# A stream of operands that runs ahead by free memory, and raw weights loaded a pass ahead of their sums

## The chip, the cores and the metric

The kernel runs on one core of one Trainium2 chip. Its five engines work from queues of their own and wait for each other by semaphores: TensorE (PE) multiplies, VectorE (DVE) and ScalarE (ACT) work on elements, GpSimd (POOL) does a little arithmetic and issues most stores, SyncE (SP) issues the loads. The metric is the device time of one execution in microseconds, lower is better.

## The reference

Four residual sublayers in turn: Fourier mixing, gated feed-forward, mixing, feed-forward, each on a layer-normalised input of 2048 rows and 512 columns, all in float32.

```
a = z @ dft_hid_re.T ; b = z @ dft_hid_im.T        # z = layernorm(x), 2048 x 512
x = x + (dft_seq_re @ a - dft_seq_im @ b)          # 2048 x 2048 matrices
x = x + (gelu(z @ w_gate) * (z @ w_up)) @ w_down   # 512 x 1792, 1792 x 512
```

## The kernel before

**Arithmetic.** A float32 operand v is divided into two parts that TensorE takes at its full rate: hi, a rounded copy written by ACT (L110), and lo = v - hi, written by DVE (L111). Each product is then three matmuls, hi by hi, hi by lo and lo by hi (`mm3`, L144 to L146), on operands of 128 x 128 and 128 x 512. The large products are done in blocks of two by two with seven products instead of eight. This needs sums and differences of operands ahead of the products (`plus`, L135, and `minus`, L132, both on DVE) and of results after them; the latter read PSUM by L135 (DVE) or are copied out of it by L139 (ACT). Such an instruction, which frees a PSUM bank that a later product needs, is called an evacuation below. The first block of layer 0 uses plain float32 matmuls instead (L551), and transposes stand at L454.

**Memory.** SBUF is 102 slots of 128 x 512 (`Slots`): `get` takes the slot that has been free longest, `put` gives one back. A load therefore waits for the last reader of the slot that it gets. Eight PSUM banks are handled in the same way.

**The stream.** All operands from outside, in the order of their use, are one list of items for the whole kernel: the rows of the sequence matrices (`ws`, A11, A12, S2, S3, A22 of four blocks in each mixing layer), the hidden matrices (`wh`), and the two parts of each down weight (`wd`). An item has its addresses and a function that makes its parts: for `ws` rows a split, for S2 rows three sums or differences and a split; a down weight was divided long before and passes as it is. `load_next` (L210) issues the loads of the next item on SP; `split_next` makes the parts of the next item, after loading up to RAW = 4 further items; `take`, called by each product, makes items up to AHEAD = 5 ahead of the one it returns:

```
    while stream["split"] <= min(n + AHEAD, len(items) - 1):
        ...
        split_next()
```

**Small jobs.** `queue` holds small jobs, one of which is run by `step()` at each product: normalising rows of x, block sums, and the preparation of weights. `weight_steps(n)` prepares gate and up weight n (14 of them): a load of the raw weight (three DMAs of `wgu`, L664 to L666, on SP behind the stream's last load), its four sums (L135, L132), and four jobs that split a piece each and store the parts (`kept`, L197, on POOL) for the three later passes, which load them ready made (`weight_load`, L712). Weights 0 and 1 are prepared in the last block of layer 0's mixing, weights 2 to 13 during the first pass of layer 1 (`geglu(0, 1)`), where `up(n)` works on weight n. There are two passes (halves of the rows) in each feed-forward layer. At the end of `up(n)` stands

```
    if making and n + 3 < NF:
        queue.extend(weight_steps(n + 3))
```
so that the load, the sums and the splits of weight n + 3 are consecutive jobs during `up(n + 1)`. Gates go through L722 to L725 (ACT, DVE, ACT, DVE) and L739 (DVE).

**Order.** A scheduler reads this program and fixes the order of the instructions on each engine before the run. On the chip each engine works through its queue strictly in that order, so an instruction whose operand is late holds up all behind it on the same engine. SP issues loads in program order.

Of the kernel before, what the change touches and what calls it, by code (L numbers as in the profile page):

```python
# [10 lines left out]
F32R = mybir.dt.float32r  # L11
# [7 lines left out]
NF = F // P  # L19
# [6 lines left out]
AHEAD = 5  # L26
RAW = 4
WARM = 16
LAG = 6
EARLY = 2  # L30
SKEW = 2
NSLOT = 102
# [6 lines left out]
def fnet_geglu(ctx: ExitStack, tc: tile.TileContext, x_in, ws, wh, wgu, wdn, out):  # L39
# [63 lines left out]
    sb = Slots(slots, "s", NSLOT)  # L103
    ps8 = Slots(psum, "p", 8)

    def f32(ap):
        return ap.bitcast(F32)
# [82 lines left out]
    wds = {f: dram.tile([P, 1024], F32, name=f"wd{f}") for f in range(NF)}  # L190

    def halves(t):
        return t[:, :512], t[:, 512:]
# [6 lines left out]
    items = []  # L200
    stream = {"loaded": 0, "split": 0, "used": 0}
    raws, parts = {}, {}

    def load_next():
        n = stream["loaded"]
        dtype, addresses, _, _ = items[n]
        raws[n] = []
        for a in addresses:
            t = sb.get(dtype)
            stream["last"] = nc.sync.dma_start(t if dtype == F32 else f32(t), a)  # L210
            raws[n].append(t)
        stream["loaded"] += 1

    def split_next():
        n = stream["split"]
        while stream["loaded"] <= min(n + RAW, len(items) - 1):
            load_next()
        parts[n] = items[n][2](*raws.pop(n))
        stream["split"] += 1

    def take():
        n = stream["used"]
        while stream["split"] <= min(n + AHEAD, len(items) - 1):
            need = items[stream["split"]][3]
            if need and need not in cs and stream["split"] > n:
                break
            split_next()
        stream["used"] += 1
        return parts.pop(n)

# [5 lines left out]
    s1s, s2s, s3s, cs, held = {}, {}, {}, {}, {}  # L236

    def as_is(v):
        return (v,)

    def make_a11(k):

# [110 lines left out]
    for layer in range(0, 4, 2):  # L353
        mix_items(layer)
        for _ in range(NB // 2):
            items.extend((F32R, halves(wds[f]), lambda *w: w, None) for _ in range(2) for f in range(NF))


    queue = []
# [147 lines left out]
    def mix(layer):  # L507
        hid, sums = {}, {}
# [69 lines left out]
                    cs[0, c] = v  # L578
            ps8.put(*side)

        chains, sides, us, ws4 = {}, {}, {}, {}

        def s2(b):
            last, fore = b == NB - 1, b < FORE[layer]
            if fore:
                chains[b] = [ps8.get() for _ in range(2)]
                if b:
                    sums[b] = [fetched((layer, b, c)) for c in range(2)]
                    cs.update({(0, c): fetched((layer, b, c, "sum")) for c in range(2)})
            chain, side = chains[b], [ps8.get() for _ in range(2)]  # L590
            sides[b] = side
            if last and layer == 0:
                queue.extend(weight_steps(0))
            for second, k in skewed():
                if second:
                    six(side, "T1", k, k == 0, k == NK - 1, "T12" if last else None)
                else:
                    six(chain, "T2", k, fore and k == 0, k == NK - 1)
            us[b] = [based(b, c, p) for c, p in enumerate(chain)]
            ws4[b] = [based(b, c, p) for c, p in enumerate(side)]  # L600

        def s3(b):
            last = b == NB - 1
            chain, side, u, w4 = chains[b], sides.pop(b), us.pop(b), ws4.pop(b)
            if last:
                queue.extend(block_steps(layer + 1, 0))
                if layer == 0:
                    queue.extend(weight_steps(1))
            for second, k in skewed():
                if second:  # L610
                    six(side, "B22", k, False, k == NK - 1, "2" if last else None)
                else:
                    six(chain, "T3", k, False, k == NK - 1)
                if not second and k == NK - 1:
                    for c in range(2):
                        plus(w4[c], w4[c], chain[c])
                        cs[1, 2 + c] = w4[c]
            for c in range(2):
                plus(u[c], u[c], side[c])
                cs[0, 2 + c] = u[c]  # L620
            ps8.put(*side)
# [27 lines left out]
    pieces = (("A11", "A12"), ("S2", "S3"), ("S1", "A22"), ("S4",))  # L649
# [4 lines left out]
    def weight_steps(n):  # L654

        src, v = [], {}

        def load():
            src.extend(sb.get() for _ in range(4))
            for i, names in enumerate((*pieces[:3], ("S4", "A21"))):  # L660
                for name, h in zip(names, half):
                    v[name] = src[i][:, h]
            with tc.issue_after(stream["last"].ins):
                nc.sync.dma_start(src[0], wgu[n, :, :512])  # L664
                nc.sync.dma_start(v["A22"], wgu[n, :, 512:768])
                nc.sync.dma_start(v["A21"], wgu[n, :, 768:])  # L666

        def sums():
            plus(v["S1"], v["A21"], v["A22"])
            minus(v["S2"], v["S1"], v["A11"])  # L670
            minus(v["S3"], v["A11"], v["A21"])
            minus(v["S4"], v["A12"], v["S2"])

        def divide(i):
            def run():
                to = wblocks[n][:, i * 1024:min((i + 1) * 1024, 7 * 512)]
                p = wparts.setdefault(n, {"tiles": []})
                if i < 3:
                    t = split_slot(src[i])
                    kept(to, t)  # L680
                    for name, h in zip(pieces[i], half):
                        p[name] = (t[0][:, h], t[1][:, h])
                else:
                    t = (split_side(v["S4"]),)
                    nc.gpsimd.dma_start(to, f32(t[0]))
                    p["S4"] = (t[0][:, half[0]], t[0][:, half[1]])
                p["tiles"] += t
                sb.put(src[i])
            return run

        return [load, sums] + [divide(i) for i in range(len(pieces))]

    def down_weight_steps(f):

# [33 lines left out]
    def geglu(w, layer):  # L728
# [30 lines left out]
                yield  # L759
            sb.put(*hs, *v)  # L760

        making = layer == 1 and w == 0


        chain, side, c11, u, w4 = {}, {}, {}, {}, {}
# [1 line left out]
        def product(n, ps, an, bn, start, stop):  # L767
            if making:
                step()
            hi, lo = wparts[n][an]  # L770
            for c in range(2):
                cut = slice(c * P, (c + 1) * P)
                mm3(ps, (hi[:, cut], lo[:, cut]), blocks[bn, c], start and c == 0, stop and c == 1)
# [15 lines left out]
                sb.put(v)  # L789

        def up(n, down):
            product(n, chain[n], "S2", "T2", False, True)
            u[n] = copied(chain[n])
            next(down, None)
            side[n] = ps8.get()
            product(n, side[n], "S1", "T1", True, True)
            w4[n] = copied(side[n])
            next(down, None)
            first(n + 1)
            product(n, chain[n], "S3", "T3", False, True)  # L800
            v = w4.pop(n)
            plus(v, v, chain[n])
            finished(n, 1, 1, v)
            sb.put(v)
            next(down, None)
            product(n, side[n], "S4", "B22", False, True)
            v = u.pop(n)
            plus(v, v, side[n])
            ps8.put(side.pop(n))
            finished(n, 0, 1, v)  # L810
            sb.put(v)
            next(down, None)
            second(n + 1)
            product(n, chain[n], "A22", "T4", False, True)
            ps = chain.pop(n)
            if n % 2 == 0:
                v = copied(ps)
                finished(n, 1, 0, v)
                sb.put(v)
            else:  # L820
                finished(n, 1, 0, ps)
            ps8.put(ps)
            for _ in down:
                pass
            sb.put(*wparts.pop(n)["tiles"])
            if making and n + 3 < NF:
                queue.extend(weight_steps(n + 3))
            elif not making and n + 2 < NF:
                weight_load(n + 2)

        def down(f, part):
# [24 lines left out]
                x_add(layer, (w * 2 + 1) * NT + i, xrows.pop(0), acc[1][i], engine=nc.sync)  # L856

        before_mix = w == 1 and layer < 3
        if making:
            queue.extend(weight_steps(2))  # L860
        first(0)
        second(0)
        for n in range(NF):
            up(n, down_steps(n - LAG, 0) if n >= LAG else iter(()))
        for bc in list(blocks):
            sb.put(*blocks.pop(bc))
        load_rows(0)
        if before_mix:
            queue.extend((lambda k=k: first_rows(layer + 1, k)) for k in range(NK))
        for f in range(NF - LAG, NF):  # L870
            down(f, 0)
# [112 lines left out]
```

## Time and profile before

| | us |
|---|---|
| median of 3 runs (lowest, highest) | 1668.8 (1666.82, 1669.08) |
| the profiled execution | 1666.76 |
| its span, first to last instruction | 1664.9 |
| PE busy | 1650.4 |
| DVE busy | 1190.7 |
| ACT busy | 776.2 |
| median landing of a load of a `ws` row, a `wd` part | 4.0, 4.3 |

The profile is of one execution. A timeline row gives start, duration, engine, line, operation, operands and shape, and in square brackets the idle time of the engine before it and what ended that. Matmuls are drawn longer than the distance of their starts, as they overlap in the array. A row with x2 or more joins that many instructions that follow each other. L12 is line 12 of the kernel before, and `s`, `p`, `x`, `ws`, `wgu`, `wd` are slots, PSUM banks, rows of x, sequence rows, raw gate and up weights, and down weights. In the table by stretches each row is a time window with the busy time and count of each engine.

### The profile page before, as it was taken

What the parts mean: (1) busy time and instruction counts of PE and PEld (TensorE: products, weight loads), DVE (VectorE), ACT (ScalarE), POOL (GpSimd) and SP (SyncE); (2) the same over time, 40 slices, a digit from 0 to 9 for tenths busy, and PEclk for the clock granted to TensorE, in tenths of its full rate; (3) what the DMA queues carried; (4) which work ended last, traced back from release to release, by engine and by line L of the source; (5) the groups of instructions that cost most, each with busy time, mean ns of one, the idle gap of its engine ahead of it and who ended that gap; (6) DMA issues with size and microseconds to landing.
All of it is one profiled execution on the core that took longest, in us unless ns stands there. A gap on an engine that the chain in (4) does not pass through costs nothing.

```text
span 1664.9 us, 22527 instructions
## 1 busy us (share of the span) xinstructions
PE 1650.4 (99%) x7296; PEld 1359.2 (82%) x7296; DVE 1190.7 (72%) x2132; ACT 776.2 (47%) x1352; POOL 169.3 (10%) x288
## 2 busy tenths in 40 slices
PE   9999999999999999999999999999999999999999
PEld 6877788888788888888888888888888888888887
DVE  8997978687887765655898785857946556656561
ACT  7744434255565543534663333444635443444440
POOL 3212100021422110000210000000100000100000
PEclk9999999999999999999999999999999999999999
DMA  9788886778766876555665766565695559755551
GB/s 361 247 279 329 306 317 227 253 252 291 273 229 215 292 269 233 172 189 198 216 227 182 240 228 228 168 227 188 225 386 184 171 177 321 259 178 175 186 183 51
DMA packets 200726, 388.46 MB, mean 233 GB/s; under 512 B 23840, under 2 KB 27424, under 8 KB 200608
## 3 DMA queue, kind: packets, MB, share of 16 engines
q1 hardware_dynamic: 183168, 329.86, 59.1%
q0 software_dynamic: 17440, 57.16, 9.1%
q8 instruction: 58, 0.95, 0.2%
q14 instruction: 60, 0.49, 0.1%
HBM read 328.73 MB, written 58.20 MB: 232 GB/s over the span
## 4 chain that ended last, share of the span: by engine, by line
PE 93%; DVE 3%; DMA 2%; issue 1%; ACT 1%; SPq 0%; DVEq 0%; ACTq 0%
PE p L144 31%; PE p L145 30%; PE p L146 30%; DMA s<-wgu 2%; DVE s L111 1%; PE p L551 1%; PE p L454 1%; DVE s L135 1%; DMA s<-ws 1%; DVE s L132 1%; DMA s<-x 0%; DVE s L725 0%; DVE s L739 0%; DVE s L723 0%; ACT s L110 0%
## 5 line engine op out<-in xcount | busy, mean ns | idle before, releaser
L145 PE MATMUL p<-s,s 128*128 128x512 f32 x2368 | 921.7, 390 | 1.9 <-DVE s L111 1.9
L146 PE MATMUL p<-s,s 128*128 128x512 f32 x2368 | 908.6, 390 | 0.0
L144 PE MATMUL p<-s,s 128*128 128x512 f32 x2368 | 901.2, 391 | 7.0 <-DVE s L135 3.9
L110 ACT ACTIVATE s<-s 128x512 fp32r<-128x512 f32 (+1 forms) x758 | 438.0, 617 | 467.6 <-DVE s L132 98.6
L111 DVE TENSOR_TENSOR s<-s,s 128x512 fp32r<-128x512 f32 (+1 forms) x758 | 490.2, 679 | 87.1 <-ACT s L110 64.3
L144 PEld LDWEIGHTS p<-s,s 128*128 128x128 f32 x2368 | 445.0, 188 | 102.9 <-DVE s L135 5.0
L145 PEld LDWEIGHTS p<-s,s 128*128 128x128 f32 x2368 | 445.4, 188 | 95.0 <-DVE s L111 3.1
L146 PEld LDWEIGHTS p<-s,s 128*128 128x128 f32 x2368 | 445.2, 188 | 93.7 <-DVE s L111 0.7
L135 DVE TENSOR_TENSOR s<-s,p 128x512 f32<-128x512 f32 x316 | 213.0, 685 | 188.9 <-PE p L146 140.6
L139 ACT ACTIVATE s<-p 128x512 f32<-128x512 f32 x248 | 145.2, 593 | 187.4 <-PE p L146 171.4
L132 DVE TENSOR_TENSOR s<-s,s 128x512 f32<-128x512 f32 (+1 forms) x290 | 172.4, 608 | 23.4 <-DMA s<-ws 15.4
L722 ACT ACTIVATE s<-s 128x512 f32<-128x512 f32 x112 | 70.4, 630 | 91.7 <-DVE s L135 90.9
L725 DVE SCALAR_TENSOR_TENSOR s<-s,s 128x512 f32<-128x512 f32 x112 | 76.8, 690 | 38.2 <-ACT s L724 37.6
L378 POOL TENSOR_TENSOR rstd<-rstd,power 128x1 f32<-128x1 f32 x64 | 50.8, 803 | 506.7 <-DVE rstd L377 500.8
L723 DVE SCALAR_TENSOR_TENSOR s<-s,s 128x512 f32<-128x512 f32 x112 | 77.0, 690 | 33.5 <-ACT s L722 31.3
L724 ACT ACTIVATE s<-s 128x512 f32<-128x512 f32 x112 | 69.5, 627 | 25.0 <-DVE s L723 24.4
L135 DVE TENSOR_TENSOR s<-s,s 128x512 f32<-128x512 f32 (+1 forms) x78 | 50.1, 645 | 38.5 <-DMA s<-ws 22.1
L169 POOL DMA_DIRECT2D x<-s x48 | 26.1, 543 | 443.8 <-DVE s L135 440.8
L382 ACT ACTIVATE s<-s,shift,rstd 128x512 f32<-128x512 f32 x64 | 50.4, 811 | 36.5 <-DVE shift L380 32.1
L739 DVE SCALAR_TENSOR_TENSOR s<-s,s 128x512 f32<-128x512 f32 x84 | 58.0, 690 | 1.6
L197 POOL DMA_DIRECT2D wb<-s x84 | 45.2, 540 | 121.6 <-ACT s L110 85.1
L373 DVE BATCH_NORM_STATS2 st<-s 128x6 f32<-128x512 f32 x64 | 42.7, 689 | 19.8 <-DMA s<-x 19.8
(32 smaller groups left out, 254.6 us busy)
## 6 DMA issues: line engine op xcount, KB each, us to landing
s<-ws SPq DMA_DIRECT2D x432, 256.0 KB, 4.0
s<-wb SPq DMA_DIRECT2D x294, 256.0 KB, 4.1
s<-wd SPq DMA_DIRECT2D x224, 256.0 KB, 4.3
s<-x SPq DMA_DIRECT2D x126, 256.0 KB, 4.1
s<-wh SPq DMA_DIRECT2D x120, 256.0 KB, 4.8
wb<-s POOLq DMA_DIRECT2D x98, 256.0 KB, 3.5
x<-s POOLq DMA_DIRECT2D x48, 256.0 KB, 4.1
wd<-s POOLq DMA_DIRECT2D x28, 256.0 KB, 4.9
```

Source lines behind the costliest of these rows:

```text
L110: nc.scalar.activation(hi, src, AF.Copy)
L111: nc.vector.tensor_tensor(lo, src, f32(hi), op=ALU.subtract)
L132: nc.vector.tensor_tensor(out, a, b, op=ALU.subtract)
L135: nc.vector.tensor_tensor(out, a, b, op=ALU.add)
L139: nc.scalar.activation(v, src, AF.Copy)
L144: nc.tensor.matmul(ps, ah, bh, start=start, stop=False, skip_group_check=True)
L145: nc.tensor.matmul(ps, ah, bl, start=False, stop=False, skip_group_check=True)
L146: nc.tensor.matmul(ps, al, bh, start=False, stop=stop, skip_group_check=True)
L722: nc.scalar.activation(t, g, AF.Square)
L723: nc.vector.scalar_tensor_tensor(t, t, 1.0 / GELU_C, g, op0=ALU.add, op1=ALU.mult)
L724: nc.scalar.activation(t, t, AF.Tanh, scale=GELU_A * GELU_C)
L725: nc.vector.scalar_tensor_tensor(t, t, 1.0, g, op0=ALU.add, op1=ALU.mult)
```

## The change

The stream: `take` may make the parts of one further item, up to FAR = 14 ahead of the item it returns, if more than ROOM = 10 slots are free and the item isn't a down weight. Down weights, whose parts need no work, are loaded and held only NEAR = 2 ahead.

The weights: `weight_steps` returns its load apart from its other jobs. In the first pass of layer 1 the load of weight n + 3 is issued at the beginning of `up(n)`, and the sums and splits of weight n + 2 are queued there; before, load, sums and splits of n + 3 were queued together at the end of `up(n)`. The load of weight 2 stands at the start of the pass. The loads of weights 0 and 1 are both queued in the S2 part of layer 0's last block, with the sums and splits of weight 0 behind them; those of weight 1 are queued in the S3 part.

Both kernels issue the same instructions; their order on the engines and the slots that they use differ. Line numbers shift by 3 near the top and by about 15 further down.

```diff
+FAR = 14
+ROOM = 10
+NEAR = 2
...
     def split_next():
         n = stream["split"]
         while stream["loaded"] <= min(n + RAW, len(items) - 1):
+            if stream["loaded"] > n + NEAR and items[stream["loaded"]][2] is whole:
+                break
             load_next()
...
             if need and need not in cs and stream["split"] > n:
                 break
+            if items[stream["split"]][2] is whole and stream["split"] > n + NEAR:
+                break
             split_next()
+        m = stream["split"]
+        if n + AHEAD < m <= min(n + FAR, len(items) - 1) and len(sb.free) > ROOM:
+            if items[m][2] is not whole and (items[m][3] is None or items[m][3] in cs):
+                split_next()
         stream["used"] += 1
         return parts.pop(n)
...
+    def whole(*parts):
+        return parts
...
-            items.extend((F32R, halves(wds[f]), lambda *w: w, None) for _ in range(2) for f in range(NF))
+            items.extend((F32R, halves(wds[f]), whole, None) for _ in range(2) for f in range(NF))
...
         def s2(b):
             if last and layer == 0:
-                queue.extend(weight_steps(0))
+                opening_weights.update((n, weight_steps(n)) for n in range(2))
+                queue.extend([opening_weights[0][0], None, opening_weights[1][0], None, *opening_weights[0][1]])
...
         def s3(b):
                 if layer == 0:
-                    queue.extend(weight_steps(1))
+                    queue.extend(opening_weights[1][1])
...
-        return [load, sums] + [divide(i) for i in range(len(pieces))]
+        return load, [sums] + [divide(i) for i in range(len(pieces))]
...
-        making = layer == 1 and w == 0
+        making = {}
+        if layer == 1 and w == 0:
+            making.update((n, weight_steps(n)) for n in range(2, NF))
+            making[2][0]()
...
         def up(n, down):
+            if n + 3 in making:
+                making[n + 3][0]()
+            if n + 2 in making:
+                queue.extend(making[n + 2][1])
             product(n, chain[n], "S2", "T2", False, True)
...
-            if making and n + 3 < NF:
-                queue.extend(weight_steps(n + 3))
-            elif not making and n + 2 < NF:
+            if not making and n + 2 < NF:
                 weight_load(n + 2)
...
-        if making:
-            queue.extend(weight_steps(2))
```

More of the change, by code (lines that the diff above doesn't have):

```diff
@@ L579, in a12 @@
             ps8.put(*side)
-        chains, sides, us, ws4 = {}, {}, {}, {}
+        chains, sides, us, ws4, opening_weights = {}, {}, {}, {}, {}
         def s2(b):
```

## The prediction

> **What bounds the kernel now.** I read the page's first part, then what PE waited for, then PE's timeline around each of those waits, then the table by stretches, and last the queues behind the waits.
>
> ```profile
> PE 1650.4 (99%) x7296; PEld 1359.2 (82%) x7296; DVE 1190.7 (72%) x2132; ACT 776.2 (47%) x1352; POOL 169.3 (10%) x288
> ```
> ```profile
> engine line waited for: us in total, times, longest us
> PE p L144 <- DVE s L135: 3.9, 3, 2.3
> PE p L144 <- ACT s L139: 2.5, 3, 1.9
> PE p L145 <- DVE s L111: 1.9, 2, 1.1
> PE p L144 <- ACT s L110: 0.6, 1, 0.6
> ```
> PE is the bound: 99% busy, and outside the first microseconds its waits add up to 8.9 us in nine places. Only these can be won, since both kernels issue the same instructions. PE's timeline shows the places and what each really costs:
>
> ```profile
> 88.26 0.50 PE L145 MATMUL p<-s,s 128*128 128x512 f32 x1 [0.83 <-DVE s L111]
> ...
> 109.54 0.74 PE L144 MATMUL p<-s,s 128*128 128x512 f32 x2 [0.58 <-ACT s L110]
> ...
> 128.63 0.50 PE L145 MATMUL p<-s,s 128*128 128x512 f32 x1 [1.12 <-DVE s L111]
> ...
> 203.33 0.80 PE L144 MATMUL p<-s,s 128*128 128x512 f32 x1 [2.30 <-DVE s L135]
> ...
> 206.46 0.40 PE L145 MATMUL p<-s,s 128*128 128x512 f32 x1
> ...
> 208.09 0.40 PE L145 MATMUL p<-s,s 128*128 128x512 f32 x1
> ...
> 211.95 0.39 PE L144 MATMUL p<-s,s 128*128 128x512 f32 x1
> ...
> 356.62 0.50 PE L144 MATMUL p<-s,s 128*128 128x512 f32 x1 [1.02 <-DVE s L135]
> ...
> 441.27 0.50 PE L144 MATMUL p<-s,s 128*128 128x512 f32 x1 [0.47 <-ACT s L139]
> ...
> 444.55 0.50 PE L144 MATMUL p<-s,s 128*128 128x512 f32 x1 [1.85 <-ACT s L139]
> 445.61 0.79 PE L144 MATMUL p<-s,s 128*128 128x512 f32 x1 [0.56 <-DVE s L135]
> ...
> 449.01 0.40 PE L144 MATMUL p<-s,s 128*128 128x512 f32 x1
> ...
> 552.40 0.50 PE L144 MATMUL p<-s,s 128*128 128x512 f32 x1 [0.18 <-ACT s L139]
> ```
> From 208.09 to 211.95 lie 17 matmuls: one starts every 0.227 us, though each is drawn 0.39 long. So a stall costs 0.16 more than the idle time in brackets: 8.91 + 9 x 0.16 = 10.35 us. After two of them PE also restarts slowly: seven matmuls from 203.33 to 206.46 take 3.13 us instead of 1.59, and eight from 445.61 to 449.01 take 3.40 instead of 1.82, together 3.1 us. All that can be won is thus about 13.5 us: 3.0 us by 130, 4.0 at 203, 1.2 at 356, 5.0 at 441 to 449, 0.3 at 552.
>
> The table by stretches (times from:to, then busy us and count of PE, PEld, DVE, ACT, POOL, the granted clock, DMA share, GB/s) tells why:
>
> ```profile
> 41.60:83.20 41.60, 41.60 (x186) 34.43 (x185) 41.15 (x86) 31.04 (x57) 10.27 (x8) 1.00 0.75 247
> 83.20:124.90 41.70, 40.29 (x177) 32.73 (x176) 40.62 (x69) 19.15 (x35) 7.56 (x14) 1.00 0.80 279
> 124.90:166.50 41.60, 40.48 (x179) 33.19 (x178) 31.65 (x52) 18.14 (x32) 11.86 (x22) 1.00 0.89 329
> 166.50:208.00 41.50, 39.20 (x167) 32.02 (x166) 40.42 (x68) 17.82 (x31) 6.48 (x12) 0.96 0.84 307
> ...
> 560.00:1664.00 1104.00, 1101.27 (x4906) 912.16 (x4905) 720.58 (x1255) 484.66 (x836) 52.90 (x88) 1.00 0.63 212
> ```
> DVE is full from 41.6 to 124.9 and from 166.5 to 208, with 10 us idle between: there a PE stall is a place in DVE's queue. From 560 on DVE has a third of its time free and PE has no wait of the list above. Between 403 and 446 the cause is another:
>
> ```profile
> 418.45 0.69 DVE L111 TENSOR_TENSOR s<-s,s 128x512 fp32r<-128x512 f32 x1 [4.80 <-ACT s L110]
> ...
> 436.98 0.43 DVE L135 TENSOR_TENSOR s<-s,s 128x256 f32<-128x256 f32 x1 [4.68 <-DMA s<-wgu]
> ```
> ```profile
> 430.78 7.73 DMA s<-wgu
> ```
> DVE idles 4.80 and 4.68 us at the head of its queue, for a raw gate and up weight that has not landed (the first through ACT's split of it); the chain of waits runs through that transfer. The evacuations queued behind are late at 441 to 446.
>
> **The change, part by part.** The instructions are the same ones in another order, so I counted, on both kernels' instruction lists, how far each operand that PE needs has moved on its producer's queue and how far its matmul has moved on PE. A DVE instruction of 512 columns counts 0.60 us:
>
> ```profile
> 360.14 0.69 DVE L373 BATCH_NORM_STATS2 st<-s 128x6 f32<-128x512 f32 x1
> 360.74 0.68 DVE L135 TENSOR_TENSOR s<-s,p 128x512 f32<-128x512 f32 x1
> ```
>
> *Raw weights a pass earlier.* Weights 2 to 13 of the first GeGLU are loaded about a pass ahead of their sums. The last load of weight 5 was issued here, when its slot came free:
>
> ```profile
> 432.67 0.72 SPq L664 DMA_DIRECT2D s<-wgu  x1
> ```
> In the new order it waits for a matmul that ran 14 us before that, and the loads of weights 2 to 4 are released by work that ran 7 to 12 us before theirs. With the weights there earlier, DVE does their sums where it now idles 4.80 and 4.68 us, and so reaches the evacuations of 441 to 446 up to 9.5 us sooner; these have moved back by only 1.0 us of work, two to three places. The 5.0 us and the 0.3 us at 552 go: **-5.3 us**.
>
> What is late next? The sums of weights 7 to 13 still stand at the head of DVE soon after their loads. In 446 to 560 DVE waits for them today without hurting PE:
>
> ```profile
> DVE s L135 <- DMA s<-wgu: 7.8, 5, 2.9
> DVE s L132 <- DMA s<-wgu: 4.3, 3, 2.6
> ```
> In the new order I count waits of 1.5 to 3 us with at least 1.6 us of slack for the evacuations behind: nothing on the path at the median landing, the fourth rival beyond it.
>
> *Weights 0 and 1 and x0 near 335 to 365.* Weight 1's three loads and its sums move from about 390 into the stretch from 333 where DVE is nearly full. Two rows tell the room there: the evacuation of row 360.74 above, which ended at 361.42, and the matmul that needs it, the second of the two here, at 365.40:
>
> ```profile
> 365.18 0.62 PE L144 MATMUL p<-s,s 128*128 128x512 f32 x2
> ```
> Its slack was 3.99 us. In the new order that matmul stands 38 places earlier, 8.6 us, while its evacuation (no. 568 on DVE, now 564) has only 2.9 us less work ahead. It is late by 8.6 - 2.9 - 3.99 = 1.7 us; and as today's stall of 1.2 us at 356 lies ahead of that matmul and goes, by 2.9 us. That is longer than the 2.30 us after which PE restarted slowly, so 1.5 us come on top. Ends: 0 (DVE has had time to catch up) and 4.4; I take 4.4, since row 203.33 is the nearest in length. Against today's 1.2: **+3.2 us**.
>
> A rule bears on that restart. The microsecond after the idle 2.30 us, with the granted clock behind the five engines:
>
> ```profile
> 203.00:204.00 1.00, 0.67 (x2) 0.58 (x3) 1.00 (x3) 0.00 (x0) 0.49 (x1) 0.51 0.73 293
> ```
> The Trainium skill, "TensorE: Matmul & The Clock Gate", section "Why this matters for your kernels", sets the limit for a halved clock at idle gaps of about 3 us. The trace shows 0.51 after 2.30 us, and the measurement decides; by the page's limit a stall of 2.9 us would restart at full speed, and the sum would be 1.5 us lower (rival 5).
>
> *The stream up to fourteen items ahead, 41 to 130.* The split that PE waited for at 88 moves from no. 190 to 172 on DVE, 10.6 us less work ahead: gone. The one at 109 (ACT) has 2.3 us less, the one at 128 2.4 us less against 1.3: gone. But block 0's later operands pulled ahead stand before earlier ones. An example is the split no. 223, the second of this DVE row, and its matmul:
>
> ```profile
> 106.73 1.33 DVE L111 TENSOR_TENSOR s<-s,s 128x512 fp32r<-128x512 f32 x2
> ```
> ```profile
> 111.48 0.39 PE L145 MATMUL p<-s,s 128*128 128x512 f32 x1
> ```
> The split ends at 108.06, so its slack was 3.4 us; its place on DVE stays, its matmul comes 18 places (4.1 us) earlier: late by 0.7 us. Two neighbours are late by 1.1 and 1.3 by the same count, and the 1.0 us of the stall at 88 that is gone comes on top: 2.3 us in three pieces, none long enough for a slow restart. Ends 0 and 4. So 3.0 becomes 2.3: **-0.7 us**.
>
> *130 to 208.* Block 1's operands are loaded 2 to 16 us earlier. The evacuation of 203.33 stays where it was (no. 358, now 357), but its matmul stands 16 places, 3.6 us, later on PE, against 2.5 us of stall: **-4.0 us** with its restart. In its stead one split (no. 335, now 345) has 6.0 us more work ahead, and a matmul 1.8 us later; the 10 us in which DVE idles in 124.90 to 166.50 cover it. Without that cover it costs up to 3.4 us; I take 0.
>
> *Down weights two items ahead instead of five; the start.* How long a load takes at worst is shown by the nearest kind, the raw weights of L664:
>
> ```profile
> DMA to landing us min/median/max: 2.5/4.7/7.2
> ```
> The shorter lead still leaves 80 matmuls, 18 us, ahead of their use, so 0. At the start the first block's loads go one place ahead of x4 and later rows, 0 to 0.5 us: **+0.3**.
>
> **Sum**: -5.3 + 3.2 - 0.7 - 4.0 + 0.3 = -6.5 us. The profiled execution took 1666.8, so 1660.3; it was 2.0 us under the median of 1668.8, which gives **1662.3**.
>
> **The rivals.**
> 1. *Nothing new is late*: DVE, freed of its waits, reaches 335 to 365 and 97 to 105 in time. For it speaks the idle DVE time in 124.90 to 166.50; against it that DVE is full just before both places. 13.5 - 1.5 = 12 us: 1657.
> 2. *The delays only change place*: besides my 4.4 and 2.3 us the split no. 345 costs its 3.4 and restarts slowly (1.5): -6.5 + 4.9 = -1.6, 1667.2.
> 3. *It does not run ahead*: loads wait for slots anyway, and asking earlier does not free one.
>
> ```profile
> SPq L210 <- PE p L146: 311.8, 201, 7.9
> ```
> Then only places change: 1668 to 1669. Against it: the loads' releasers in the new order are earlier matmuls.
>
> 4. *Slower: the weights' sums block DVE.* A sum at the head of DVE waits for a load issued shortly before; evacuations stand behind. With 1.6 us of slack it costs PE nothing up to a landing of 4.7 + 1.6 = 6.3 us. At 7.2 each of the twelve weights stalls PE by 0.9: 10.8 us, 1673; the change is slower than today from 0.55 us for each. Today's waits of 7.8 and 4.3 us left PE alone, which speaks against. The Trainium skill, "DMA: Bandwidth & Descriptors", section "Latency and other measured facts", allows memory access 2 us at high load instead of 0.2, which as an estimate would reach 6.5; the transfers here run at 0.6 to 0.9 of the engines' time and land as that row says, mostly sooner.
> 5. *The stall near 350 restarts at full speed*, because PE's idle time ends just short of what the clock reacts to: 1.5 us less, 1660.8. Row 203.33 speaks against it, row 128.63 with 1.12 us and no slow restart for it. This is what the page on the clock gate would have.
>
> **How the numbers follow.** My forecast has 0.38 (1659 to 1665), the first rival 0.22, the second and third 0.16 together, the fourth 0.12, the fifth 0.12. Runs of this kernel differ by 0.14%, so about 0.2%, 3.3 us, can be told from no change: below 1665.5 is faster. Forecast, first and fifth rival give faster 0.72, the second and third same 0.16, the fourth slower 0.12. The range leaves out the fourth and the ends of the others: 1655.5 (all but the start and a remnant of 0.2 won) to 1668.5.
>
> **What would show it.** Right: no PE wait on L139's line near 441 to 446, none at 203; DVE's waits on wgu before 446 under 4 us; a PE stall of 2 to 3 us behind an evacuation near 350 with the clock at 0.5 after it; small PE waits on L111's line near 97 to 105; nothing after 560. Wrong: PE waits between 446 and 560 behind DVE waits on wgu (rival 4), a stall near 185 (rival 2), or load waits where they are today (rival 3).

## The result: 0.22% slower

Over 17 runs of each kernel the changed one takes 1672.1 us (median, 1666.2 to 1674.4) and the one before 1668.0 (1663.4 to 1671.8): ratio 1.0022, 95% interval 1.0012 to 1.0032. I had forecast 1662.3, and 1655.5 to 1668.5 as the range. The profiled execution of the changed kernel took 1673.5 us, 6.7 more than that of before.

The page's first part and PE's waits, after:

```profile
PE 1650.8 (99%) x7296; PEld 1359.6 (81%) x7296; DVE 1191.2 (71%) x2132; ACT 777.3 (46%) x1352; POOL 173.8 (10%) x288
```
```profile
PE p L147 <- DVE s L138: 6.9, 2, 5.8
PE p L148 <- DVE s L114: 6.1, 5, 3.1
PE p L147 <- ACT s L113: 2.2, 3, 0.9
```
The work is the same; PE's waits in the steady part grew from 8.9 to 15.2 us. (Lines have moved: L147 to L149 are the three matmuls, L113 and L114 the split, L135 and L138 the difference and the sum, L142 the copy out of PSUM.) PE's timeline shows where:

```profile
99.75 0.50 PE L147 MATMUL p<-s,s 128*128 128x512 f32 x1 [0.76 <-ACT s L113]
...
107.27 0.50 PE L148 MATMUL p<-s,s 128*128 128x512 f32 x1 [3.11 <-DVE s L114]
...
153.50 0.50 PE L147 MATMUL p<-s,s 128*128 128x512 f32 x1 [1.06 <-DVE s L138]
...
195.89 0.50 PE L148 MATMUL p<-s,s 128*128 128x512 f32 x1 [0.39 <-DVE s L114]
...
352.33 0.50 PE L147 MATMUL p<-s,s 128*128 128x512 f32 x1 [0.88 <-ACT s L113]
...
363.42 0.77 PE L147 MATMUL p<-s,s 128*128 128x512 f32 x1 [5.84 <-DVE s L138]
...
368.58 0.39 PE L149 MATMUL p<-s,s 128*128 128x512 f32 x1
...
869.98 0.50 PE L148 MATMUL p<-s,s 128*128 128x512 f32 x1 [1.27 <-DVE s L114]
...
979.16 0.96 PE L147 MATMUL p<-s,s 128*128 128x512 f32 x3 [0.54 <-ACT s L113]
...
981.14 0.50 PE L148 MATMUL p<-s,s 128*128 128x512 f32 x1 [1.02 <-DVE s L114]
```
Counted from start to start, less 0.227 us for each matmul, the stalls of over 0.25 us (slow restarts included) sum to 15.2 us before and 21.6 after. Without them the last matmul would end at 1646.1 and 1646.4: the stalls are the whole difference, but for 0.3 us of the start.

| place | before, us | after, us |
|---|---|---|
| up to 130 | 3.3 | 4.7 |
| 150 to 208 | 4.0 | 2.0 |
| 351 to 369 | 1.3 | 10.2 |
| 440 to 553 | 5.7 | 0 |
| 868 and 978 to 981 | 0 | 3.6 |
| others, small | 0.8 | 1.1 |

So the stalls that I expected to go did go at 203 and from 441 to 552; what came in their place is far larger than I had counted, above all at 357 to 369.

DVE is late there, and its timelines show where it lost the time. After:

```profile
310.85 1.45 DVE L138 TENSOR_TENSOR s<-s,s 128x512 f32<-128x512 f32 x2 [5.96 <-DMA s<-ws]
...
333.20 0.69 DVE L138 TENSOR_TENSOR s<-s,s 128x512 f32<-128x512 f32 x1 [4.50 <-DMA s<-ws]
...
337.92 0.69 DVE L138 TENSOR_TENSOR s<-s,s 128x512 f32<-128x512 f32 x1 [1.97 <-DMA s<-ws]
...
362.60 0.68 DVE L138 TENSOR_TENSOR s<-s,p 128x512 f32<-128x512 f32 x1
```
and before, in the same stage:

```profile
305.85 0.69 DVE L135 TENSOR_TENSOR s<-s,s 128x512 f32<-128x512 f32 x1 [1.18 <-DMA s<-ws]
...
325.58 0.69 DVE L135 TENSOR_TENSOR s<-s,s 128x512 f32<-128x512 f32 x1 [2.05 <-DMA s<-ws]
...
331.21 0.42 DVE L135 TENSOR_TENSOR s<-s,s 128x256 f32<-128x256 f32 x1 [2.81 <-PE p L146]
```
The evacuation of row 362.60 ends at 363.28, and PE starts at 363.42. From 338 to there DVE doesn't pause: it had come late into the stage, after waiting 5.96, 4.50 and 1.97 us for rows of `ws`. SP's timeline shows when their loads went out. After, then before:

```profile
300.02 3.89 SPq L213 DMA_DIRECT2D s<-wh  x7
304.60 13.21 SPq L213 DMA_DIRECT2D s<-ws  x12
317.90 6.35 SPq L165 DMA_DIRECT2D s<-x  x2
324.35 0.38 SPq L213 DMA_DIRECT2D s<-ws  x1
...
327.54 0.33 SPq L213 DMA_DIRECT2D s<-ws  x1
```
```profile
301.22 0.33 SPq L210 DMA_DIRECT2D s<-wh  x1
302.36 13.05 SPq L210 DMA_DIRECT2D s<-ws  x12
315.96 3.12 SPq L162 DMA_DIRECT2D s<-x  x4
320.04 3.25 SPq L210 DMA_DIRECT2D s<-ws  x4
```
The rows behind the wait of 5.96 us go out from 304.60 on, straight behind seven loads of `wh`, and DVE has them at 310.85; before they went out from 302.36 on, behind a single one, and DVE had them at 305.85. Why the seven stand there is not shown. Behind the other two stands a wait of SP: the four loads of x rows are issued in 3.1 us before, and after, the second of them (row x9) goes out at 323.93, when the evacuation that reads its slot has finished. The `ws` loads behind it in SP's queue go out 4 to 5 us later than before. SP's waits before loads of x rows from 290 to 340 (sum, times, longest), of which x9's is the 5.6:

```profile
SPq L165 <- DVE s L138: 5.9, 2, 5.6
```

### The profile page after: what moved, and what is told of

The parts are those of the page before. It is cut to its first block, busy times and chain, and to the rows that moved or that the text cites. A ratio compares the mean times of both kernels' runs of the same rounds, so it can differ in the third digit from the quotient of the medians.

```text
span 1671.6 us, 22532 instructions
## 1 busy us (share of the span) xinstructions
PE 1650.8 (99%) x7296; PEld 1359.6 (81%) x7296; DVE 1191.2 (71%) x2132; ACT 777.3 (46%) x1352; POOL 173.8 (10%) x288
## 4 chain that ended last, share of the span: by engine, by line
PE 91%; DVE 4%; DMA 3%; issue 1%; ACT 0%; POOL 0%; SPq 0%; DVEq 0%; POOLq 0%; ACTq 0%
PE p L148 30%; PE p L149 30%; PE p L147 30%; DVE s L114 2%; DMA s<-ws 2%; DMA s<-x 1%; PE p L565 1%; PE p L468 1%; DVE s L138 1%; DVE s L135 1%; DVE st L387 0%; DMA s<-wdn 0%; DMA x<-s 0%; ACT s L113 0%; POOL rstd L392 0%
## 5 line engine op out<-in xcount | busy, mean ns | idle before, releaser
L147 PE MATMUL p<-s,s 128*128 128x512 f32 x2368 | 902.0, 391 | 9.1 <-DVE s L138 6.9
L149 PE MATMUL p<-s,s 128*128 128x512 f32 x2368 | 905.2, 390 | 0.0
L113 ACT ACTIVATE s<-s 128x512 fp32r<-128x512 f32 (+1 forms) x758 | 440.2, 618 | 470.4 <-DVE s L135 106.8
L114 DVE TENSOR_TENSOR s<-s,s 128x512 fp32r<-128x512 f32 (+1 forms) x758 | 489.0, 675 | 93.6 <-ACT s L113 70.2
L147 PEld LDWEIGHTS p<-s,s 128*128 128x128 f32 x2368 | 444.9, 188 | 104.1 <-ACT s L113 9.9
L149 PEld LDWEIGHTS p<-s,s 128*128 128x128 f32 x2368 | 445.1, 188 | 93.2 <-issue 0.5
L138 DVE TENSOR_TENSOR s<-s,p 128x512 f32<-128x512 f32 x316 | 212.5, 683 | 190.0 <-PE p L149 143.2
L142 ACT ACTIVATE s<-p 128x512 f32<-128x512 f32 x248 | 145.7, 594 | 181.2 <-PE p L149 166.0
L135 DVE TENSOR_TENSOR s<-s,s 128x512 f32<-128x512 f32 (+1 forms) x290 | 170.9, 603 | 19.5 <-DMA s<-ws 16.3
L392 POOL TENSOR_TENSOR rstd<-rstd,power 128x1 f32<-128x1 f32 x64 | 54.8, 866 | 512.8 <-DVE rstd L391 490.0
L138 DVE TENSOR_TENSOR s<-s,s 128x512 f32<-128x512 f32 (+1 forms) x78 | 49.8, 640 | 44.2 <-DMA s<-ws 30.0
```

Source lines behind the costliest of these rows:

```text
L113: nc.scalar.activation(hi, src, AF.Copy)
L114: nc.vector.tensor_tensor(lo, src, f32(hi), op=ALU.subtract)
L135: nc.vector.tensor_tensor(out, a, b, op=ALU.subtract)
L138: nc.vector.tensor_tensor(out, a, b, op=ALU.add)
L142: nc.scalar.activation(v, src, AF.Copy)
L147: nc.tensor.matmul(ps, ah, bh, start=start, stop=False, skip_group_check=True)
```

## The experiments

Each run is compared with the kernel before on the same chip; the ratios have 95% intervals. Stalls are those of PE in one profile, counted as above. The edits are abridged, and partly told in words. The runs that fix an order by `issue_after` have the lines of the matmuls two further down (L149 to L151), and those on DVE's order also the sums (L140).

**The parts.** The stream part alone (the weights as before):

```diff
+FAR = 14 ; ROOM = 10 ; NEAR = 2, and all of the change in split_next and take
```


> The change's stream part alone (the further item while more than 10 slots are free, down weights only 2 ahead); all weights are prepared as in the kernel before. Theory A (the stream that runs ahead makes the new stalls: the changed kernel's waits near 98 to 104, 152, 195, 868 and 980, 10.7 us together, and by held slots much of the one at 357): PE's stalls of before up to 208 (7.0 us) are replaced by those 10.7, the 5.4 us at 441 to 552 stay, and about 3 us stand near 355: 1673 to 1676, slower than before by 5 to 8. Theory B (the opening weights, moved into DVE's full stretch, make the 357 stall and with it the whole loss): no long stall near 357, 1671 to 1672.

The weights part alone:

```diff
+opening_weights ... ; making[n + 3][0]() ; queue.extend(making[n + 2][1])
```


> The weights part alone (opening weights 0 and 1 and the loads of weights 2 to 13 a pass ahead of their sums); the stream as before. Theory A: the stalls at 441 to 552 go (5.4 us), those up to 208 stay as before (7.0 us), and near 355 at most 2 to 3 us: about 1663 to 1664. Theory B: the stall near 357 is there with 5 us or more and its slow restart: 1668 or above.

Of the weights part, the first pass of layer 1 alone:

```diff
+making[n + 3][0]() ; queue.extend(making[n + 2][1])      # weights 0 and 1 as before
```


> Only the loads of weights 2 to 13 a pass ahead of their sums; opening weights and stream as before. Both theories: the 5.4 us at 441 to 552 go and nothing else moves, 1662.6. If it is not under 1665, the gain I counted for this step was never there.

The changed kernel without the opening weights:

```diff
-queue.extend([opening_weights[0][0], None, opening_weights[1][0], None, *opening_weights[0][1]])
+queue.extend([opening_weights[0][0], *opening_weights[0][1]])      # S2; weight 1 as a whole in S3
```


> The changed kernel with weights 0 and 1 prepared as before (weight 1 loaded in the S3 part). Theory A: the stall near 357 loses only what weight 1's sums and splits put ahead of the evacuation (4 sums of 0.33 us and 3.5 splits of 0.60, 3.4 us): 1668 to 1670. Theory B: the whole stall with its restart goes, 8 us or more: 1664 or less.

Measured: 1.0025 (1.0016 to 1.0034), 1.0001 (0.9992 to 1.0011), 0.9986 (0.9977 to 0.9995) and 1.0023 (1.0014 to 1.0032). The stream part is the loss, as theory A has it, though 4 us and not 5 to 8; but the opening weights make a stall near 357 by themselves too, as theory B has it. The rows of the stream part alone, and of the weights part alone:

```profile
106.05 0.50 PE L148 MATMUL p<-s,s 128*128 128x512 f32 x1 [3.12 <-DVE s L114]
...
359.93 0.76 PE L147 MATMUL p<-s,s 128*128 128x512 f32 x1 [5.23 <-ACT s L113]
```
```profile
359.38 0.47 PE L147 MATMUL p<-s,s 128*128 128x512 f32 x1 [3.76 <-DVE s L138]
```
Without the opening weights the changed kernel's stall there is as long as with them (next row), so I had both theories too simple: either cause is enough.

```profile
360.86 0.77 PE L147 MATMUL p<-s,s 128*128 128x512 f32 x1 [5.44 <-ACT s L113]
```
The loads a pass ahead gained 2.3 us and not the 5.4 that both theories expected. One stall of 441 was left:

```profile
444.23 0.50 PE L147 MATMUL p<-s,s 128*128 128x512 f32 x1 [2.46 <-DVE s L138]
```
The stream part alone had none at 438 to 447, although it loads those weights as before. What it does there is to hold fewer down weights.

**The slots.** Only the shorter hold of the down weights, and this with the loads a pass ahead:

```diff
+NEAR = 2 and its two conditions for `whole` items; no FAR
```


> Only the shorter hold of the down weights: loaded and held 2 ahead instead of 5 or more; no further item, weights prepared as before. The kernel with the whole stream part had no stall at 441, though its raw weights were loaded as in the kernel before. Theory C (the stall at 441 is one of slots: down weights that lie ready take the slots that raw weights 2 to 13 wait for): the stalls at 441 to 552 go, 5 to 6 us, and those up to 208 and the 1.3 at 355 stay: 1658 to 1659 against a before of 1664. Rival D (the further item or a reordering of it took that stall away): no change, 1664.

> Shorter hold of the down weights and the loads of weights 2 to 13 a pass ahead of their sums; opening weights and stream otherwise as before. Theory C: the two ways remove the same stall, so little more than by the shorter hold alone, 1657.5 to 1659. Rival D: as with the weights' loads alone, 1661 to 1662.

Measured: 0.9960 (0.9947 to 0.9973) and 0.9955 (0.9941 to 0.9968), 1657.9 us for the second. Both times are as theory C has them, and rival D is out. The execution of the first that was profiled took 5958 us, so its profile can't show the place of the gain. The stream part's profile fits theory C: DVE's longest wait for a raw weight from 400 to 446 is there

```profile
423.63 0.42 DVE L138 TENSOR_TENSOR s<-s,s 128x256 f32<-128x256 f32 x1 [3.15 <-DMA s<-wgu]
```
instead of 4.80 and 4.68 us. That the shorter hold works by its slots, and not by the order that the planner then makes, is likely but not shown apart. The second run's waits are in the places of before (86 to 130, 201, 355), with one of 0.3 us near 1006, and none between 440 and 560:

```profile
PE p L147 <- DVE s L138: 3.4, 3, 2.3
PE p L148 <- DVE s L114: 2.0, 2, 1.0
...
PE p L147 <- ACT s L113: 1.4, 1, 1.4
```
The stream part is thus two edits with opposite signs. Its 1.0025 against the 0.9960 of the shorter hold puts the further item by itself, as an estimate from the two ratios, at +0.65% or 11 us.

Fewer slots with the kernel before, and loads no further ahead with the stream part:

```diff
-NSLOT = 102
+NSLOT = 98
```


> The kernel before with 98 slots instead of 102, nothing else changed. Theory C' (the further item does its harm by the slots that it holds: a load gets a slot that comes free later and stands in SP's queue ahead of others, as x9's did at 318 to 324 in the changed kernel): stalls of 3 us and more appear near 103 and near 357 without any split moved ahead on purpose, 4 us or more slower in sum. Rival E (the harm is the order on DVE: the split of a further item stands ahead of work that is due): those two places stay within 1.5 us of before, and the time within 3 us.

```diff
-RAW = 4
+RAW = 3      # on the stream part alone
```


> The stream part alone, but with raw operands loaded 3 instead of 4 items beyond the last one whose parts are made, so that loads run as far ahead as before the change while splits are made one item earlier. Theory C': at most a slot or two more are held than before, the stalls near 103 and 357 shrink to 2 us or less each, and with the gain at 441 the time is 1659 to 1662. Rival E: the splits stand where they stood in the stream part alone, so the stalls of 5 and 8 us stay and the time is 1667 to 1669.

Measured: 1.0061 (1.0047 to 1.0074) and 1.0017 (1.0008 to 1.0026). Four slots fewer brought the stalls near 103 and 357, as C' expected:

```profile
105.48 0.50 PE L145 MATMUL p<-s,s 128*128 128x512 f32 x1 [1.96 <-DVE s L111]
...
352.26 0.50 PE L145 MATMUL p<-s,s 128*128 128x512 f32 x1 [1.92 <-DVE s L111]
...
355.85 0.80 PE L144 MATMUL p<-s,s 128*128 128x512 f32 x1 [2.34 <-DVE s L135]
```
But giving the slots back did not take them away (3.5 us near 103 and 7.1 near 356 were left, rival E's numbers). Slots alone don't explain it.

**Orders.** In all kernels with the long stall up to then, PE's order near 355 had changed: S4's products, which need an evacuation and a fresh split, stood ahead of S3's. So I pinned PE's order:

```diff
+with tc.issue_after(last S3 matmul): six(side, "B22", k, ...)      # layer 0, last block
```


> The changed kernel with one constraint: in S3 of layer 0's last block, the S4 matmuls of step k are queued on PE behind the S3 matmuls that stand ahead of them in the program. In the kernel before, S3's products stand first there (from no. 1472 on PE) and S4's from no. 1510; in the changed kernel S4's from 1472 and S3's from 1486; here S3's again from 1472, S4's from 1500. Theory F (the stall near 357 is made by that exchange on PE, an S4 product that waits for its evacuation and split while S3's are ready): the stall of 6.6 us and its restart of 2.4 shrink to 2 us or less, and the time is 6 to 8 us under the changed kernel's, 1.000 to 0.998 of before. Rival C' (loads that wait for slots make DVE late there, whatever PE's order): the stall stands elsewhere in the stage with the same length, and the time stays at 1.002 of before.

```diff
-AHEAD = 5, FAR = 14
+AHEAD = 6, no FAR      # NEAR = 2, weights as before
```


> Shorter hold of the down weights, and AHEAD = 6 instead of the rule for a further item; weights prepared as before. In the program's order of the changed kernel the stream is 7 items ahead where it was 6, never 14, since each call takes one item and makes at most one further. Theory G (the rule amounts to one item more): as the stream part alone, 1.0015 to 1.0035 of before, with stalls near 103 and 357. Rival H (the rule does something else as well, by its count of free slots or at its end): under 1.000.

```diff
-AHEAD = 5
+AHEAD = 4      # on the version with the shorter hold and the loads a pass ahead
```


> Shorter hold of the down weights, the loads of weights 2 to 13 a pass ahead, no further item, and AHEAD = 4 instead of 5. S4's products stand ahead of S3's at no. 1472 and 1486. Theory F: a stall of 4 to 8 us near 357 although fewer slots are held, so 3 us or more slower than with AHEAD = 5: 1.000 to 1.003. Rival C' (slots): no such stall, 0.995 or less.

```diff
-if n + AHEAD < m <= ... and len(sb.free) > ROOM: ... split_next()
+while len(sb.free) > ROOM: the same, as often as it holds      # opening weights as before
```


> The stream part and the loads of weights 2 to 13 a pass ahead, opening weights as before, and the rule repeated as long as more than 10 slots are free, so that the stream really runs up to 14 items ahead. S3's products stand first at no. 1472, S4's at 1505. Theory F: no stall over 2 us near 357 in spite of the most slots held of all kernels; what is left are stalls in the stretches where DVE is full: 0.997 to 1.002. Rival C': stalls near 103 and 357 larger than with one item, 1.004 or more.

Measured: 1.0044 (1.0031 to 1.0058), 1.0025 (1.0015 to 1.0035), 1.0045 (1.0031 to 1.0059), 1.0027 (1.0017 to 1.0037). Theory F, that PE's order is the cause, fell with the first of them: S3's products came first and PE stood just as long, now for the evacuation of their bank:

```profile
363.52 0.80 PE L149 MATMUL p<-s,s 128*128 128x512 f32 x1 [7.55 <-DVE s L138]
```
With four items ahead there is a stall near 357 (4.0 us and a restart of 1.7) and a longer one near 100; with really up to fourteen there is one of 2.2 us near 357, and others at 33, 105 and 888 to 900. So the amount of look-ahead by itself decides neither place. AHEAD = 6 gives the ratio of the stream part, 1.0025: the rule for a further item amounts to one item more (theory G).

What does decide shows when the profiles are laid side by side. PE could be at the matmul in question (no. 1472, counted from 0 without the 32 that open the kernel) 96 matmuls, 21.8 us, after its no. 1376; the evacuation that it waits for takes 0.7 us. All times in us, from PE's no. 1376. DVE's no. 482 starts 31.8 us before that in every kernel of the table but the one with 98 slots, so the table divides the time from there (with 98 slots, from the same moment) to the evacuation into DVE's work and its idle time:

| kernel | place of the evacuation on DVE | its start | DVE's work | DVE idle | stall up to 363 |
|---|---|---|---|---|---|
| before | 559 | 22.2 | 46.2 | 7.8 | 1.3 |
| loads a pass ahead | 559 | 21.8 | 46.1 | 7.4 | 0.9 |
| with the shorter hold | 559 | 22.0 | 46.2 | 7.6 | 1.0 |
| weights part | 565 | 25.2 | 48.3 | 8.6 | 4.2 |
| stream part, RAW = 3 | 563 | 25.4 | 48.6 | 8.6 | 4.5 |
| 98 slots | 561 | 25.8 | 48.7 | 8.8 | 4.8 |
| stream part | 562 | 26.3 | 47.7 | 10.4 | 5.4 |
| changed | 564 | 28.8 | 47.9 | 12.7 | 7.7 |
| PE's order pinned | 567 | 29.6 | 49.7 | 11.7 | 8.3 |
| AHEAD = 6 | 563 | 29.6 | 48.3 | 13.0 | 8.6 |

In each row the stall is the evacuation's start, plus 0.7, less 21.8, within 0.5 us. Against before, the weights part is 3.0 us later, 2.1 by work and 0.8 by idle time; the stream part 4.1 us, 1.5 by work and 2.6 by idle time; the changed kernel 6.6 us, 1.7 by work and 4.9 by idle time. That the idle time depends on how far raw operands are loaded ahead shows in the stream part: with RAW = 3 the evacuation stands one place later and the idle time is 1.8 us less. To split the two terms, one more edit:

```diff
+with tc.issue_after(last evacuation of S2): the products of S3      # DVE work made there waits its turn
```


> The changed kernel; all DVE work that S3 of layer 0's last block makes (splits, sums, the small jobs run there) is queued on DVE behind the four evacuations of S2. The evacuation that PE waits for moves from no. 564 to 558 on DVE, 6 instructions or 3.5 us less ahead of it; PE's order stays (S4's products at 1472, S3's at 1486). In 13 profiles the length of the stall is the end of that evacuation less the time at which PE could be there. Theory K (the stall is the sum of DVE's work ahead of the evacuation and of DVE's idle time while loads wait for slots): the part for the work goes, 7.7 us near 351 to 357 become 4 to 4.5, and the time falls by 3 to 4 us, to 1.000 of before. Rival L (only late loads matter, the place in DVE's queue is filled by waiting anyway): the stall stays at 7 us or more.

> The kernel with the evacuations first, and raw operands loaded 3 instead of 4 items beyond the last one made, so that loads hold no more slots than before the change. Theory K: DVE's idle time in the 40 us before the stage falls from 15 us to about 11 as in the stream part alone with that edit, and the stall near 357 to 1.5 us or less without a slow restart; in time 0.997 to 1.000 of before. Rival M (the idle time is not of the slots): the stall is as long as in the run with the evacuations first alone, 4 us or more.

> A version meant to beat both: shorter hold of the down weights, loads of weights 2 to 13 a pass ahead, no further item, and in every block of both mixing layers S3's DVE work queued behind S2's evacuations. Those near 201 and 355 move 3 to 5 and 7 instructions forward on DVE. Theory K: the stall at 201 (2.4 us and 1.7 of restart in the version without this) and the one at 355 (1.0) go, and the time is 2 to 5 us under that version's, 0.992 to 0.994 of before. Rival: work that is put off (the splits for S3) is late in their stead, 0.996 or more.

The three runs are this edit on the changed kernel, the same with RAW = 3, and the edit in all mixing blocks of the version with the shorter hold and the loads a pass ahead. Measured: 1.0004 (0.9996 to 1.0013), 1.0012 (1.0001 to 1.0022) and 0.9966 (0.9953 to 0.9979). The first agrees with theory K: the evacuation started at 24.8 instead of 28.8, with 44.3 us of work and still 12.2 of idle time ahead of it, and the waits were now

```profile
351.76 0.73 PE L149 MATMUL p<-s,s 128*128 128x512 f32 x2 [0.46 <-ACT s L113]
...
355.89 0.50 PE L150 MATMUL p<-s,s 128*128 128x512 f32 x1 [0.37 <-DVE s L114]
...
359.32 0.77 PE L149 MATMUL p<-s,s 128*128 128x512 f32 x1 [2.24 <-DVE s L140]
```
3.8 us and a restart of 1.6 instead of 7.7 and 2.4. Half of the changed kernel's long stall thus goes with DVE's order; DVE's work is now less than before the change, and what is left is the late loads.

The second run bears on that other half. With the evacuation at the same place (no. 558) DVE's idle time fell from 12.2 to 10.0 us, the evacuation started at 22.7, and the stall at this matmul fell from 3.8 to 1.7 us without a slow restart, close to the 1.5 of theory K; so about half of the extra idle time hangs on the raw operands loaded ahead, and what makes the rest stays open. The time did not follow. PE now waited for a later evacuation in the same stage,

```profile
361.02 0.50 PE L149 MATMUL p<-s,s 128*128 128x512 f32 x1 [2.21 <-DVE s L140]
```
so that the stalls there sum to 4.4 us, and new ones came at 860 to 874 (6.4 us).

The third took the stalls at 201 and 355 away as expected (0.3 us and none; PE's waits in its profile sum to 3.8 us against 6.8 in the version without the edit), but not the time: its ratio can't be told from 0.9955, and it is in the range of the rival. Of the 3.8 us, 2.0 are new waits at 369 to 375, which fits the rival: work that is put off is late in turn. The profile of the version without the edit is its slowest execution, 1661.3 us, so its median may have fewer stalls than its profile; I leave this open. Both beat the kernel before by 0.3 to 0.5%.

## Why the prediction was wrong, step by step

- *What bounds it*: right. PE's stalls are the whole difference.
- *Raw weights a pass earlier, -5.3*: the stalls from 441 to 552 went, and 5.7 us with them. The cause was credited wrongly: the loads ahead are worth 2.3 us alone, the shorter hold of the down weights, which I had put at 0, 6.7 (0.0040 of 1665), and both together 7.5. One sign that I had named did not come: DVE's waits for raw weights from 400 to 446 sum to 5.2 us, not to under 4, though in shorter pieces than the 4.80 and 4.68 of before.

```profile
DVE s L138 <- DMA s<-wgu: 5.2, 3, 2.3
```
- *335 to 365, +3.2*: the step that failed. Place, evacuation and slow restart were as written, but the stall was 7.7 us, not 2.9, and the restart 2.4, not 1.5: +8.9. The count of DVE's work held: from its no. 482 to this evacuation it fell by 3.2 us, from 51.1 (to no. 568) to 47.9 (to no. 564), where I had 2.9. What failed is the other term, which I had put at no change without a reason: that DVE arrives in the stage as it did before. It was idle for 12.7 us on the way instead of 7.8, and these 4.9 us are what the stall was longer by. They are waits for `ws` rows that were loaded late: one load that waits for its slot (x9) holds all loads behind it on SP's queue, and with fewer raw operands loaded ahead about half of the extra idle time goes (above); what makes the other half, the late `ws` rows behind seven loads of `wh` among it, stays open. The note in the third rival, that loads wait for slots, stood beside this and was not carried into the sum.
- *41 to 130, -0.7*: +1.4. The places were right (98 to 108, DVE's L114), 4.7 us and not 2.3. DVE was idle for 2.1 us by then instead of 0.5: 0.3 for a `ws` row and 1.3 for a split of ACT, which had itself stood for 7 us because a raw down weight (`wdn`) was late.

```profile
96.72 0.69 DVE L135 TENSOR_TENSOR s<-s,s 128x512 f32<-128x512 f32 x1 [0.31 <-DMA s<-ws]
98.70 1.30 DVE L114 TENSOR_TENSOR s<-s,s 128x512 fp32r<-128x512 f32 x2 [1.28 <-ACT s L113]
```
```profile
98.03 3.76 ACT L113 ACTIVATE s<-s 128x512 fp32r<-128x512 f32 x7 [6.97 <-DMA s<-wdn]
```
  That weight's load went out at 91.52 us, and at 85.42 before:

```profile
91.52 0.38 SPq L715 DMA_DIRECT2D s<-wdn  x1
```
```profile
85.42 0.33 SPq L700 DMA_DIRECT2D s<-wdn  x1
```
  This is 1.6 us of the 2.4 that the count was short by; the rest is not divided further.
- *130 to 208, -4.0*: the stall at 203 went, but 1.3 us at 153 and 0.7 at 195 came: -2.0. The one at 195 is the split no. 345, which I took at 0 with 3.4 as its bound: it cost 0.7.
- *Down weights, 0*: nothing late, but a gain, likely by the slots that it frees, missed (above).
- *After 560, nothing*: 3.6 us at 868 and 978 to 981, in layer 2's mixing, where I had looked at the slack in the new order with the loads' times of before.
- *The start, +0.3*: the matmul that starts at 38.8 us before starts at 39.5 us; in the sum of stalls 0.3 is left over.
- *Sum*: -5.7 + 8.9 + 1.4 - 2.0 + 3.6 + 0.3, and 0.3 in small ones, is 6.8; the two profiled executions differ by 6.7.
- *The rivals*: the second (delays only change place) was nearest by its mechanism. I had its worst at 1667.2, since it too took loads to be in time. The fourth, my only slower one, did not happen: PE has no wait at all from 446 to 560. "Up to fourteen items ahead", as I put it, is not what the change does: a call of `take` takes one item and makes at most one further, so the stream runs seven items ahead where it ran six.

A word on the clock rule that I weighed. By the Trainium skill, "TensorE: Matmul & The Clock Gate", section "Why this matters for your kernels", gaps up to about 3 us would leave the clock alone. Here no length separates the cases. The stretch after the 3.11 us of the changed kernel, at full clock, and that after the 3.12 us of the stream part alone, at half:

```profile
108.00:109.00 1.00, 1.00 (x6) 0.79 (x6) 1.00 (x3) 0.63 (x1) 0.07 (x1) 1.00 0.00 0
```
```profile
107.00:108.00 1.00, 1.00 (x4) 0.73 (x3) 1.00 (x3) 0.96 (x2) 0.00 (x0) 0.50 0.00 0
```
The same page says, in the section "What's actually happening", that the window over which activity is watched runs freely; two equal gaps with different ends agree with that.

## What to carry to other kernels

When a second engine is full for a stretch, a stall of the first is the time at which that engine comes to one instruction, and this has two terms: the work queued ahead of it, and the idle time that it has had on the way. Counting a new order gives only the first; the second must be found by following each load's slot to its last reader and SP's queue behind it. Prefetching further takes slots, and here one item more was dearer than the waits it removed, while holding ready-made operands for a shorter time gained 0.4% by itself.

## What I had not expected of the machine and the order

- SP's loads do not go out in the program's order either: the planner orders them too. By the kernels' instruction lists, in the stream part alone the row of an item (b0's A11, k = 1) was loaded at 89.9 us, after rows for k = 3 and 5; before it went out at 77.3. The section on the kernel before says "program order" and is wrong there.
- Of six changes to the look-ahead or the slots (AHEAD 4 and 6, the further item, up to fourteen, RAW = 3, 98 slots) all six were 0.17 to 0.61% slower than before, although five of them had the shorter hold, which alone is 0.4% faster. The order that the planner makes for DVE's full stretches differs each time.
- The clock can halve after 2.30 us of idle PE and stay full after 3.11 us.
